# Where the receptance product R of a step is placed, in a convolution and channel-mix kernel on one core

## The chip, the cores and the metric

The kernel runs on one core of one Trainium2 chip. The metric is device time in microseconds (us) of that core, from the first to the last instruction with what starting and ending the program adds; lower is better. The profile is one execution taken by the hardware profiler; its span is a little shorter than the time that is measured without it. Five engines work side by side, each on its own list of instructions: TensorE (PE, with its weight loads PEld), VectorE (DVE), ScalarE (ACT), GpSimd (POOL) and SyncE (SP, which here only issues transfers).

## The reference

The input x has 8 sequences of 4160 positions with 192 channels. First comes a causal convolution of 7 taps, with the softmax of 8 rows of weights (one for each group of 24 channels). Its result y goes through a channel mix, in which each position is also mixed with the position before it:

```python
xk = mu_k * y + (1.0 - mu_k) * y_prev
xr = mu_r * y + (1.0 - mu_r) * y_prev
k = np.maximum(xk @ w_k, 0.0)          # 192 -> 1024
v = k * k @ w_v                        # 1024 -> 192
r = 1.0 / (1.0 + np.exp(-(xr @ w_r)))  # 192 -> 192
out = r * v
```

## The kernel before

**Layout.** Two sequences are worked on together (a pair p of four), one in partitions 0 to 63 and one in 64 to 127 of the 128. The convolved y of a pair lies transposed, channels by positions, in the tile yT.

**Steps.** A step s is 512 positions of a pair. The first pair begins with a step of 256 (step 0) and ends with one of 256 (step 8); the other pairs have eight steps of 512. The last 64 positions of all pairs form a last step, number 33 (LAST). In a step, VectorE makes the difference `d` of neighbouring positions (`diff`, L480), scales it by mu (`scale`, L516) and adds y (`add_y`, L522), once into xk and once into xr. The tiles xk and xr have two buffers each, which the steps take in turn.

**Products.** K of a step comes in 8 slots (4 in a step of 256 positions); a slot is 128 rows of the 1024 for both sequences, in one PSUM tile of two banks. `k_mm` (L542) multiplies, `k_relu` (L554, ScalarE) takes it into the tile k_sb, which has four buffers, and `k_square` (L568, VectorE) squares it into k2. V and R are made for 256 positions at a time (j counts them): `r` (L599) and `r_out` (L610, the sigmoid on ScalarE), `v_rows` (L630) in two halves, and `v_out` (L646, VectorE), which multiplies V by R and starts the stores.

**PSUM.** All of K, R, V and the convolution share one ring of four PSUM tiles (`ring`, tag "k"). A tile is held from its first matmul until ScalarE or VectorE has read it. V's is held longest, until `v_out` at the beginning of the next bundle.

**Bundles.** The order of the work is written out by hand and kept by each engine. Four K slots make a bundle; there are 65, counted from 0, so that a step of 512 positions has two bundles and step 8 has bundle 15 alone. `first_bundle[s]` and `last_bundle[s]` say where a step's K lies. V of a pair of halves is due one bundle after its step's last K, one V in a bundle: this is `vb` in the list `quads`. A bundle from the fourth on (`bundle_rest`) runs in this order: the squares left over, the lists `mix_a`, V's output of the bundle before, two K with their relus, `mix_b`, two squares, `mix_c`, the third K, the R products of list `rq`, V's first half, a square, the fourth K, convolution pieces in some bundles, V's second half. The sigmoids of the list `rs` stand ahead of V's first half in bundles with convolution pieces, and behind it in the others.

Into these lists go, for a step s with first bundle fb, the difference in the bundle fb - 2 as a rule, xk's work in fb - 1, and the scaling of xr in `mix_c` of fb - 1, then in fb:

```python
at(mix_c, fb - 1, scale, s, 1, 0)
at(mix_a, fb, scale, s, 1, 1)
```

R of the pair (s, j) is put into a bundle by one line, and V by `vb`:

```python
b = min(vb, last_bundle[s] + 1 + j) if s else vb
at(rq, b, r, s, j)
at(rs, b, r_out, s, j)
```

Around step 8 this gives:

| pair (s, j) | vb | bundle of R before |
|---|---|---|
| (6, 0), (6, 1) | 13, 14 | 13, 14 |
| (7, 0), (7, 1) | 15, 16 | 15, 16 |
| (8, 0) | 17 | 16 |
| (9, 0), (9, 1) | 18, 19 | 18, 19 |

**Convolution.** Most of y is made by TensorE from the loaded x (L302), copied out by ScalarE (L319), written to a buffer in DRAM (L424) and read back transposed into yT (L432). In the first bundles the convolution of the first pair still goes on.

Of the kernel before, what the change touches and what calls it, by code (L numbers as in the profile page):

```python
# [14 lines left out]
def kernel(  # L15
# [56 lines left out]
    T0, LAST = S - TAIL, len(steps) - 1  # L72
# [11 lines left out]
    first_bundle = [bundle_of[st[3]] for st in steps]  # L84
    last_bundle = [bundle_of[st[3] + st[4] - 1] for st in steps]
# [202 lines left out]
    def conv_tiles(g, c):  # L288

        nb = groups[g][2]  # L290
        if c == 0:
            ys[g] = two.tile([P, GB, 2 * D], BF16, tag="y", name="y")
        ps = ring.tile([P, 2, BANK], FP32, tag="k", name="ps_c")
        conv_ps[g, c] = ps
        m = nb // 2
        banks = ps[:, :, 0 : m * 4 * G].rearrange("p i (m s c) -> p i m s c", m=m, s=2)
        for k in range(2):
            h = 2 * c + k
            for i in range(2):
                q = slice(i * Q, (i + 1) * Q)  # L300
                for j in range(2):
                    nc.tensor.matmul(  # L302
                        out=banks[j * Q : (j + 1) * Q, i, :, :, k * G : (k + 1) * G],
                        lhsT=toe[q, h, q],
                        rhs=xbs[g][q, j * m : (j + 1) * m, :, h * G : (h + 1) * G],
                        start=True,
                        stop=True,
                    )

    def conv_tiles_out(g, c):  # L310

        m = groups[g][2] // 2
        ps = conv_ps.pop((g, c))
        y = ys[g]
        c0, c1 = 2 * c * G, 2 * (c + 1) * G
        cuts = [c0] + [a for a in range(Q, D, Q) if c0 < a < c1] + [c1]
        for a, b in zip(cuts, cuts[1:]):
            d = a // Q * 2 * Q + a % Q
            nc.scalar.copy(  # L319
                out=bass.AP(  # L320
                    tensor=y.tensor,
                    offset=y.offset + d,
                    ap=[y.ap[0], [m * 2 * D, 2], [2 * D, m], [Q, 2], [1, b - a]],
                ),
                in_=bass.AP(
                    tensor=ps.tensor,
                    offset=ps.offset + a - c0,
                    ap=[ps.ap[0], [BANK, 2], [4 * G, m], [2 * G, 2], [1, b - a]],
                ),
            )  # L330
# [195 lines left out]
    def k_mm(n, cs=range(NC)):  # L526


        s, j = slots[n]
        L = steps[s][2]  # L530
        xk = xks[s]
        if cs[0] == 0 and n not in k_ps:
            k_ps[n] = ring.tile([P, 2, BANK], FP32, tag="k", name="ps_k")
        ps = k_ps[n]
        nf = STEP // L

        for c in cs:
            for f in range(nf):
                fs = slice((j * nf + f) * P, (j * nf + f + 1) * P)
                for i in range(2):  # L540
                    r = slice(i * Q, (i + 1) * Q)
                    nc.tensor.matmul(  # L542
                        out=ps[:, i, f * L : (f + 1) * L],
                        lhsT=wk[r, c, fs],
                        rhs=xk[r, c, :L],
                        start=c == 0 and f == 0,
                        stop=c == NC - 1 and f == nf - 1,
                    )

    def k_relu(n):  # L550
        ps = k_ps.pop(n)
        k_sb = four.tile([P, 2 * STEP], BF16, tag="k_sb", name="k_sb")
        k_sbs[n] = k_sb
        nc.scalar.activation(out=k_sb, in_=ps.rearrange("p a b -> p (a b)"), func=AF.Relu)  # L554

    def k_square(n):
        s, j = slots[n]
        L = steps[s][2]
        k_sb = k_sbs.pop(n)
        if j == 0:  # L560
            k2s[s] = three.tile([P, NF, 2 * STEP], BF16, tag="k2", name="k2")
        nf = STEP // L
        i = k_sb
        o = k2s[s][:, j, :]
        if nf > 1:
            i = k_sb.rearrange("p (b f t) -> p f b t", b=2, f=nf)
            o = k2s[s][:, j * nf : (j + 1) * nf, 0 : 2 * L].rearrange("p f (b t) -> p f b t", b=2)
        nc.vector.tensor_tensor(out=o, in0=i, in1=i, op=ALU.mult)  # L568
# [3 lines left out]
    vb = 1  # L572
    for s, (p, t0, L, n0, ns) in enumerate(steps):
        for j in range(L // 256):
            vb = max(vb, last_bundle[s]) + 1
# [44 lines left out]
    def v_rows(s, j, half, ks=(0, 1)):  # L620

        if half == 0:
            v_ps[s, j] = ring.tile([P, 2, BANK], FP32, tag="k", name="ps_v")[:, :, 0 : 2 * D]
        for k in ks:
            for f in range(NF):
                for i in range(2):
                    q = slice(i * Q, (i + 1) * Q)
                    bank = (i + half) % 2
                    t = tile_of(s, j, 2 * bank + k)
                    nc.tensor.matmul(  # L630
                        out=v_ps[s, j][:, bank, k * D : (k + 1) * D],
                        lhsT=k2s[s][q, f, t * P : (t + 1) * P],
                        rhs=wv[q, f, :],
                        start=half == 0 and k == 0 and f == 0,
                        stop=half == 1 and k == 1 and f == NF - 1,
                    )
        if half == 0:
            nc.scalar.clobber_nop([nc.scalar.lower_ap(v_ps[s, j])])
# [4 lines left out]
    def v_out(s, j):  # L643
        p, t0, L, _, _ = steps[s]
        o_sb = three.tile([P, 4, D], FP32, tag="o_sb", name="o_sb")
        nc.vector.tensor_tensor(  # L646
            out=o_sb.rearrange("p (b t) d -> p b (t d)", b=2),
            in0=v_ps.pop((s, j)),
            in1=r_sbs.pop((s, j)),
            op=ALU.mult,  # L650
        )
        for st in range(2):
            c = t0 + 2 * j * P
            nc.sync.dma_start(
                out=out[2 * p + st, c : c + 2 * P, :].rearrange("(m p) d -> p m d", p=P),
                in_=o_sb[:, 2 * st : 2 * st + 2, :],
            )
# [24 lines left out]
    early, rq, rs, xt, mix_a, mix_b, mix_c, vq, late = ({} for _ in range(9))  # L682

    def at(table, b, fn, *a):
        table.setdefault(b, []).append((fn, a))
# [7 lines left out]
    for g, (p, base, nb, fb, on_pe) in enumerate(groups):  # L693
# [12 lines left out]
        if g > 4:  # L706

            b = {5: 1, 6: 2, 7: 7}.get(g)
            b = first_bundle[first_step[p]] + (-15, -11, -7, -3)[(g - 6) % 4] if b is None else b
# [30 lines left out]
        if s == LAST - 1 or s < LAST and steps[s + 1][0] > p:  # L740
            at(late, fb - 1, keep_tail, p)
    for s, j, vb in quads:
        b = min(vb, last_bundle[s] + 1 + j) if s else vb
        at(rq, b, r, s, j)
        at(rs, b, r_out, s, j)
        if s == LAST:
            at(late, vb, v_last, s, j)
        else:
            vq.setdefault(vb, []).append((s, j))

    def run(table, b):
        for fn, a in table.get(b, ()):
            fn(*a)
# [114 lines left out]
    def bundle_rest(b, ns):  # L868

        units = xt.get(b, [])  # L870
        quad = vq[b][0]
        for n in bundles[b - 1][2 if b == 3 else 3 :]:
            k_square(n)
        run(mix_a, b)
        if b > 3:
            v_out(*vq[b - 1][0])
        k_mm(ns[0])
        k_relu(ns[0])
        k_mm(ns[1])
        k_relu(ns[1])  # L880
        run(mix_b, b)
        k_square(ns[0])
        k_square(ns[1])
        run(mix_c, b)
        k_mm(ns[2])
        k_relu(ns[2])
        run(rq, b)
        if units:
            run(rs, b)
        v_rows(*quad, 0)  # L890
        if not units:
            run(rs, b)
        k_square(ns[2])
        k_mm(ns[3])
        k_relu(ns[3])
        for u in units:
            conv_tiles(*u)
            conv_tiles_out(*u)
        v_rows(*quad, 1)
        run(late, b)  # L900
# [87 lines left out]
```

## Time and profile before

| | |
|---|---|
| time, median of 3 | 417.65 us (417.5 to 418.0) |
| span of the profiled execution | 415.7 us, TensorE clock 0.998 of full |
| TensorE busy | 404.4 us, 97% |
| TensorE weight loads busy | 301.3 us, 72% |
| VectorE busy | 369.5 us, 89% |
| ScalarE busy | 354.9 us, 85% |
| one K matmul, one V or R matmul (mean) | 367 ns, 243 ns |
| relu, sigmoid (ScalarE) | 1036 ns, 821 ns |
| square, V's output (VectorE) | 687 ns, 952 ns |

Lines of the timeline give the start and the length in us, the engine, the line of the code, the operation with the tile that it writes and those that it reads, how many instructions are joined in the line, and in brackets how long the engine stood idle before it and what it waited for. The ends of matmuls are modelled and they overlap, so their distances are best taken from start to start. The chain of waits is the chain of work that ended last, followed back from the end; its lines give start, length and what ran or waited there.

### The profile page before, as it was taken

The page shows a single profiled execution, that of the slowest core. Times are in us where ns is not written, and L with a number is a line of the kernel's source. Part 1 is how long each engine was busy: PE and PEld are TensorE (multiplying, and loading weights), DVE is VectorE, ACT ScalarE, POOL GpSimd, SP SyncE. Part 2 cuts the span into 40 slices and gives each one's busy share as a digit, 9 for nine tenths or more (in the row PEclk, how much of TensorE's full clock was granted, in tenths as well). Part 3 has the DMA queues.
Part 4 walks back from the last instruction along what each step waited for, and adds up shares of the span by engine and source line. Part 5 has one row for each costly group of instructions (what it writes and reads, how often), then busy time and mean ns, then how long its engine had stood idle before and what let it go on. Part 6 is the DMA issues. An engine that isn't in the chain of part 4 may idle for free.

```text
span 415.7 us, 16804 instructions
## 1 busy us (share of the span) xinstructions
PE 404.4 (97%) x7349; PEld 301.3 (72%) x7350; DVE 369.5 (89%) x671; ACT 354.9 (85%) x429; POOL 65.2 (16%) x102
## 2 busy tenths in 40 slices
PE   7899999999889999999999999999999999999996
PEld 5567767777667777767777777777777777777895
DVE  5989799999699999989989999998989899999973
ACT  6899988888868889988888988888898888787781
POOL 8750023021040200304031020303100000000000
PEclk9999999999999999999999999999999999999999
DMA  9999989969559795999759797796962726411223
GB/s 148 175 191 213 187 184 213 241 133 193 151 102 231 137 225 139 155 191 155 192 122 229 180 148 195 108 235 131 204 168 80 209 73 160 121 53 65 79 79 114
DMA packets 137657, 65.58 MB, mean 158 GB/s; under 512 B 87388, under 2 KB 137584, under 8 KB 137584
## 3 DMA queue, kind: packets, MB, share of 16 engines
q1 hardware_dynamic: 95840, 48.42, 44.6%
q0 software_dynamic: 40944, 15.53, 32.9%
q8 instruction: 57, 0.93, 0.9%
q10 hardware_dynamic: 800, 0.57, 0.5%
q14 instruction: 16, 0.13, 0.1%
HBM read 31.62 MB, written 37.09 MB: 165 GB/s over the span
## 4 chain that ended last, share of the span: by engine, by line
PE 85%; DMA 5%; DVE 3%; ACT 2%; POOL 2%; issue 1%; SPq 0%; ACTq 0%; DVEq 0%; POOLq 0%
PE ps_v L630 38%; PE ps_k L542 35%; PE ps_r L599 7%; PE ps_c L302 3%; DMA xb<-in_x_dram 2%; DMA yT<-y_dram 2%; PE ps_v L582 1%; DMA y_dram<-y 1%; DVE k L568 1%; POOL xb L136 1%; ACT k_sb L554 1%; POOL wk L208 1%; ACT y L319 1%; DVE o_sb L646 1%; DMA out_dram<-o_sb 1%
## 5 line engine op out<-in xcount | busy, mean ns | idle before, releaser
L554 ACT ACTIVATE k_sb<-ps_k 128x1024 bf16<-128x1024 f32 x260 | 253.2, 1036 | 36.8 <-PE ps_k L542 34.6
L568 DVE TENSOR_TENSOR k<-k_sb 128x1024 bf16<-128x1024 bf16 x260 | 172.9, 687 | 28.3 <-ACT k_sb L554 27.9
L542 PE MATMUL ps_k<-xk,wk 64*128 64x512 bf16 (+1 forms) x1632 | 191.1, 367 | 0.9 <-DVE xk L522 0.5
L630 PE MATMUL ps_v<-wv,k 64*128 64x192 bf16 x4032 | 188.2, 243 | 2.4 <-ACT k_sb L554 1.4
L630 PEld LDWEIGHTS <-k 64*128 64x128 bf16 x4032 | 168.0, 94 | 16.2 <-issue 7.0
L542 PEld LDWEIGHTS <-wk 64*128 64x128 bf16 x1632 | 80.3, 94 | 59.3 <-issue 1.3
L136 POOL DMA_DIRECT2D xb<-in_x_dram x62 | 45.1, 736 | 175.4 <-issue 81.5
L646 DVE TENSOR_TENSOR o_sb<-ps_v,r_sb 128x768 f32<-128x768 f32 x64 | 61.0, 952 | 3.1 <-issue 2.4
L610 ACT ACTIVATE r_sb<-ps_r 128x768 bf16<-128x768 f32 x65 | 53.2, 821 | 12.0 <-PE ps_v L630 11.3
L319 ACT CAST y<-ps_c 128x960 bf16<-128x960 f32 (+5 forms) x84 | 50.8, 686 | 0.0
L599 PEld LDWEIGHTS <-xr 64*128 64x128 bf16 x780 | 34.5, 94 | 16.0 <-issue 2.2
L599 PE MATMUL ps_r<-wr,xr 64*128 64x192 bf16 x780 | 43.1, 243 | 0.9 <-DVE o_sb L646 0.6
L516 DVE TENSOR_SCALAR xr<-d,mu 128x512 bf16<-128x512 bf16 (+1 forms) x102 | 35.1, 351 | 3.8 <-PE ps_r L599 3.8
L480 DVE TENSOR_TENSOR d<-yT 128x1536 bf16<-128x1536 bf16 (+3 forms) x37 | 31.5, 854 | 1.4 <-ACT yT L381 0.9
L522 DVE TENSOR_TENSOR xr<-xr,yT 128x1536 bf16<-128x1536 bf16 (+1 forms) x33 | 31.0, 939 | 1.1
L516 DVE TENSOR_SCALAR xk<-d,mu 128x512 bf16<-128x512 bf16 (+1 forms) x98 | 31.8, 353 | 0.1
L522 DVE TENSOR_TENSOR xk<-xk,yT 128x1536 bf16<-128x1536 bf16 (+2 forms) x34 | 30.6, 901 | 0.1
L302 PEld LDWEIGHTS <-toe 64*64 64x64 bf16 x448 | 9.6, 106 | 11.6 <-issue 10.8
L302 PE MATMUL ps_c<-xb,toe 64*64 64x240 bf16 (+1 forms) x448 | 16.6, 265 | 0.1
L464 POOL COPY y_tail<-yT 128x195 bf16<-128x195 bf16 x4 | 2.8, 698 | 65.0 <-DMA yT<-y_dram 64.9
L111 POOL MEMSET xb<- 32x384 bf16 x3 | 1.3, 423 | 43.2 <-DVE xb L109 43.2
L371 PEld LDWEIGHTS <-xb 128*32 128x32 bf16 (+3 forms) x264 | 4.6, 106 | 2.3 <-issue 1.0
(59 smaller groups left out, 65.0 us busy)
## 6 DMA issues: line engine op xcount, KB each, us to landing
out_dram<-o_sb SPq DMA_DIRECT2D x128, 192.0 KB
xb<-in_x_dram POOLq DMA_DIRECT2D x40, 240.0 KB, 8.1
y_dram<-y SPq DMA_DIRECT2D x44, 210.0 KB
y_dram<-y SPq DMA_DIRECT2D x12, 168.0 KB
xb<-in_x_dram POOLq DMA_DIRECT2D x10, 192.0 KB, 5.6
xb<-in_x_dram POOLq DMA_DIRECT2D x6, 216.0 KB, 6.9
xb<-in_x_dram POOLq DMA_DIRECT2D x6, 144.0 KB, 5.6
wk<-in_moe_w_k_dram POOLq DMA_DIRECT2D x4, 96.0 KB, 4.7
```

The lines of the kernel that those rows point to most:

```text
L136: nc.gpsimd.dma_start(out=xb[q0 : q0 + rows, lo:hi, s, :], in_=bass.AP(tensor=x.tensor, offset=x.offset + (b * S + t0 + lo * step) * D, ap ...
L302: nc.tensor.matmul(out=banks[j * Q : (j + 1) * Q, i, :, :, k * G : (k + 1) * G], lhsT=toe[q, h, q], rhs=xbs[g][q, j * m : (j + 1) * m, :, ...
L319: nc.scalar.copy(out=bass.AP(tensor=y.tensor, offset=y.offset + d, ap=[y.ap[0], [m * 2 * D, 2], [2 * D, m], [Q, 2], [1, b - a]],), in_=bas ...
L516: nc.vector.tensor_scalar(out=t[:, c, :L], in0=diffs[s][:, c, :L], scalar1=mu[:, i, c : c + 1], scalar2=None, op0=ALU.mult)
L522: nc.vector.tensor_tensor(out=o, in0=o, in1=y_of(s, sl, 0), op=ALU.add)
L542: nc.tensor.matmul(out=ps[:, i, f * L : (f + 1) * L], lhsT=wk[r, c, fs], rhs=xk[r, c, :L], start=c == 0 and f == 0, stop=c == NC - 1 and f ...
L554: nc.scalar.activation(out=k_sb, in_=ps.rearrange("p a b -> p (a b)"), func=AF.Relu)
L568: nc.vector.tensor_tensor(out=o, in0=i, in1=i, op=ALU.mult)
L599: nc.tensor.matmul(out=ps[:, i, k * D : (k + 1) * D], lhsT=xr[q, c, ts], rhs=wr[q, c, :], start=c == 0, stop=c == NC - 1,)
L610: nc.scalar.activation(out=r_sbs[s, j], in_=r_ps.pop((s, j))[:, :, 0 : 2 * D], func=AF.Sigmoid)
L630: nc.tensor.matmul(out=v_ps[s, j][:, bank, k * D : (k + 1) * D], lhsT=k2s[s][q, f, t * P : (t + 1) * P], rhs=wv[q, f, :], start=half == 0 ...
L646: nc.vector.tensor_tensor(out=o_sb.rearrange("p (b t) d -> p b (t d)", b=2), in0=v_ps.pop((s, j)), in1=r_sbs.pop((s, j)), op=ALU.mult,)
```

## The change

Two edits. The first gives R another rule: it may not be later than the two bundles in front of the first bundle of the second next step, one R in each, which is when the xr buffer is wanted again; without that bound it goes with its V, and the last step's R goes one bundle ahead of it. The second moves V's output in bundle 4, the fifth, ahead of the left-over square and of the scaling in `mix_a`, so that the PSUM tile of V is read earlier there; in all later bundles the order stays.

```diff
     for s, j, vb in quads:
-        b = min(vb, last_bundle[s] + 1 + j) if s else vb
+        b = vb - (s == LAST)
+        if 0 < s < LAST - 1:
+            b = min(b, first_bundle[s + 2] - 2 + j)
         at(rq, b, r, s, j)
         at(rs, b, r_out, s, j)
...
         units = xt.get(b, [])
         quad = vq[b][0]
+        if b == 4:
+            v_out(*vq[b - 1][0])
         for n in bundles[b - 1][2 if b == 3 else 3 :]:
             k_square(n)
         run(mix_a, b)
-        if b > 3:
+        if b > 4:
             v_out(*vq[b - 1][0])
```

## The prediction

> **What bounds the kernel now.** I read the page's first two parts, then the engines' busy time in stretches of two bundles, then the timeline of each engine where a stretch came out long, then the chain of waits. Bundles are counted from 0, so the fifth is bundle 4; R(s,j) and V(s,j) are the two products of pair j of step s.
>
> ```profile
> PE 404.4 (97%) x7349; PEld 301.3 (72%) x7350; DVE 369.5 (89%) x671; ACT 354.9 (85%) x429; POOL 65.2 (16%) x102
> ```
>
> TensorE is the bound: 97% busy. But the average hides one bad place. Each line below is two bundles, from the second half of V in one odd bundle to that in the next (11 to 13, 13 to 15, 15 to 17, 17 to 19); the columns are start and end, length, busy time of PE, PEld, DVE, ACT and POOL with their instructions, clock and transfers.
>
> ```profile
> 83.97:96.08 12.11, 12.11 (x218) 8.91 (x220) 11.11 (x22) 10.85 (x14) 4.64 (x7) 1.00 0.78 141
> 96.08:108.38 12.30, 12.29 (x242) 10.10 (x244) 11.43 (x23) 10.84 (x14) 0.00 (x0) 1.00 0.85 195
> 108.38:123.47 15.09, 12.71 (x220) 9.10 (x220) 11.22 (x21) 10.96 (x14) 4.03 (x7) 1.00 0.46 101
> 123.47:135.50 12.03, 12.03 (x218) 8.87 (x220) 11.73 (x22) 10.77 (x14) 0.41 (x1) 1.00 1.10 228
> ```
>
> The third has the same 48 K, 128 V, 24 R and 16 convolution matmuls as its neighbours and takes 3.0 us more (15.09 against 12.03 to 12.11). After 123 us the table of waits has no wait of TensorE at all, so whatever is saved ahead of that should arrive whole at the end. The timeline of the long stretch, VectorE first:
>
> ```profile
> 107.59 0.95 DVE L522 TENSOR_TENSOR xk<-xk,yT 128x1536 bf16<-128x1536 bf16 x1
> 112.38 0.35 DVE L516 TENSOR_SCALAR xr<-d,mu 128x512 bf16<-128x512 bf16 x1 [3.83 <-PE ps_r L599]
> 112.64 1.28 DVE L568 TENSOR_TENSOR k<-k_sb 128x1024 bf16<-128x1024 bf16 x2
> ...
> 114.11 0.95 DVE L646 TENSOR_TENSOR o_sb<-ps_v,r_sb 128x768 f32<-128x768 f32 x1
> ...
> 119.79 0.95 DVE L646 TENSOR_TENSOR o_sb<-ps_v,r_sb 128x768 f32<-128x768 f32 x1
> ```
>
> VectorE stands still for 3.83 us in front of the first scaling of xr for step 9. There are two xr buffers; step 9's is step 7's, and R(7,1) still has to read it. R(7,1) is bound to bundle 16, the scaling to the end of bundle 15. Behind the scaling, in order, wait the squares of bundle 15 and the V output of bundle 15. What this does to TensorE:
>
> ```profile
> 111.67 0.67 PE L599 MATMUL ps_r<-wr,xr 64*128 64x192 bf16 x12
> 112.58 0.67 PE L599 MATMUL ps_r<-wr,xr 64*128 64x192 bf16 x12 [0.25 <-ACT k_sb L554]
> 114.50 1.50 PE L630 MATMUL ps_v<-wv,k 64*128 64x192 bf16 x32 [1.24 <-ACT k_sb L554]
> ...
> 120.79 1.50 PE L630 MATMUL ps_v<-wv,k 64*128 64x192 bf16 x32 [0.89 <-DVE o_sb L646]
> ```
>
> Matmul ends are modelled, so I count from start to start. One R takes 0.50 (99.28 to 99.78), a half of V 1.32, three K blocks 1.94 (97.34 to 99.28). Against that the second R of bundle 16 is late by 0.41 (111.67 + 0.50 to 112.58), V by 1.42 (113.08 to 114.50), and V of bundle 17 by 1.07 (117.78 + 1.94 to 120.79; there is no R in bundle 17). Sum 2.9 to 3.0, the whole excess. The middle one goes through ScalarE: the relu at 113.42 waited 0.89 for a square, since its four k_sb buffers were full.
>
> The other place that the change touches is bundles 4 to 7. R of bundle 4 starts 2.33 after its first K (35.20 to 37.53) where 1.94 is usual: 0.39 of waiting for the V output. The chain of waits does not go through it:
>
> ```profile
> 37.96 4.73 DMA y_dram<-y
> ...
> 42.85 7.12 DMA yT<-y_dram
> ...
> 49.99 0.98 DVE d L480
> ```
>
> **What the Trainium skill says.** "Perfetto Trace Analysis", section on the Tensor Engine instruction, has ScalarE and VectorE as strict first-in-first-out queues, with TensorE's matmul end only estimated. The trace agrees on the first: the squares ready since about 109 us ran only at 112.64, behind the scaling. "PSUM — Partial Sum Buffer", section on engine versus sequencer instructions, says that matmuls start and complete in program order; so one R that lacks a buffer holds V and the next K blocks, as at 112.58 and 114.50. "Perfetto Trace Analysis", section on the most-contended engine, prefers weight-load busy time to matmul busy time as a measure of headroom. That is 72% here, yet the steady stretches show TensorE without a gap; I take the start-to-start times as its floor.
>
> **The change part by part: the R binding.** Worked out over all steps, the old and the new rule give the same bundle for every pair but two. Steps take two bundles, so the first bundle of step s+2, less 2, is just where R already is, except around step 8, which has 256 positions and one bundle (15). There R(7,0) goes from bundle 15 to 14, and R(7,1) from 16 to 15. R(8,0) stays in 16 and bundle 17 has none. So bundle 14 now has two R, bundle 16 one. The last step's R stays in bundle 65 (old minimum of 66 and 65, new 66 less 1). No instruction is added or removed.
>
> Gain: in bundle 15, R runs at about 105.2 and VectorE comes to the scaling at 108.5, so the wait of 3.83 goes. With it go the waits in bundles 16 and 17: 0.41 + 1.42 + 1.07 to 1.19, about 3.0 us.
>
> Cost: bundle 14 gets a second R and a second sigmoid. The R itself, 0.50 of TensorE, is only moved. For PSUM, R needs the slot of the V output (ended 98.50), the second R that of the first K (its relu ended about 99.2, R comes at 99.78) and V that of the second K (about 100.2, V comes at 100.28): no wait, with nothing to spare. The sigmoid is on the path:
>
> ```profile
> 101.38 0.81 ACT L610 ACTIVATE r_sb<-ps_r 128x768 bf16<-128x768 f32 x1 [0.24 <-PE ps_v L630]
> 102.08 1.02 ACT L554 ACTIVATE k_sb<-ps_k 128x1024 bf16<-128x1024 f32 x1
> ```
>
> The relu of the fourth K block follows 0.70 after a sigmoid. With the second R and sigmoid it starts at 102.08 + 0.50 + 0.70 = 103.3 and ends at 104.3. Behind it on VectorE stand its square, two scalings and the V output of bundle 14, whose end was 2.05 after the relu's (103.10 to 105.15), so it ends at about 106.4. R of bundle 15 took that slot: it starts at 105.20, just after 105.15, about 0.2 late. Unhindered it would come at 105.0 + 0.5 = 105.5; it waits until 106.4. That is 0.9 late where it was 0.2, a cost of 0.7.
>
> Does the lag go on? VectorE would be some 1.2 late, its xk for step 9 ends at 108.54 + 1.2 = 109.8, and the first K of bundle 16 comes at 109.65 + 1.2 = 110.9: no wait. The V output of bundle 15 ends near 112.5, R of bundle 16 comes near 112.8: no wait. Bundle 17 then has the timing of any other odd bundle, in which the V output ends 1.89 after the first K (90.96 to 92.85), against 1.94 for the matmul behind it. So the cost stays at 0.7. Its ends are 0 (the allocator gives R another slot) and 1.6 (V of bundle 14 has to take the third K's slot, whose relu ends at 101.14, and is another 0.9 late). Net: 3.0 less 0.7 is 2.3.
>
> **The V output in bundle 4.** VectorE's order there was two squares (35.06), the scaling of xk, the V output (36.53 to 37.48). Ahead of the second square and the scaling it can start near 35.7 and end at 36.65, before R would come (37.14), so R's 0.39 goes; the square loses 0.95, but its consumers are a bundle away. But the difference at 49.99 waits for the transposing read that landed at 49.97, and that chain begins with convolution copies at 34.22 and writes queued from 36.21, both of bundle 3. The output's stores, which could disturb it, were queued behind these writes (39.36, long after the output's end). The first K of bundle 7 waits for the xk made from this difference (ends 53.94, matmul 54.06). A TensorE that is 0.39 early waits 0.39 longer there. I take 0, with 0.4 as the other end.
>
> **The rivals.** *A full gain*: R of bundle 15 gets another slot, or bundle 4 arrives after all: 2.9 to 3.4 us, 414.2 to 414.8. For it: slots seem to go to what was freed first, and in bundle 16 R did not take the late V output's slot. Against: R did so in bundles 4, 7 and 15. *A new wait takes half*: the chain through the second sigmoid, or V in bundle 14, costs 1.6, or 1.2 to 2.1 with 0.4 to 0.5 to either side: 417.65 less 0.9 to 1.8, 415.9 to 416.8. For it: nothing is to spare in bundle 14. Against: the V output of bundle 13 is out at 98.50, well ahead of the first R at 99.28, so its slot should serve. *No change*: the stall only moves by one bundle, 417.0 to 418.4; against it stands that bundle 15's R comes 3 us ahead of the scaling. *Slower*: the crowded bundle 14 delays VectorE so that xk of step 9 comes late too, and the late k_sb releases stall the relus, as happened in bundle 16; three waits of 1.4, 1.4 and 1.2 in place of 3.0 would give 418.7. Against it: VectorE's lag of 1.2 is a third of the 3.83 that caused the old ones.
>
> **How the numbers follow.** 417.65 less 2.3 is 415.35, rounded to 415.3 (55%). Full gain 20%, half 12%, no change 8%, slower 5%. Faster by over 0.2% (0.84 us) are the first three, 87%. The range 414.2 to 416.8 holds these three and with them both ends of the unknown costs; no change and slower, 13%, stay outside but for the edge of the former.
>
> **What would show it.** Right: no wait of VectorE for ps_r, the stretch from bundle 15's V to bundle 17's V near 12 us, the R of bundle 15 just behind the end of the V output of bundle 14 with VectorE some 1.2 late, and the difference of step 4 still released by the transposing read near 50 us. Wrong: a wait of TensorE over 1 us between 97 and 106, any repeating gap after 123, or the first K of bundle 7 well before 54.

## The result, and the profile after

| | before | after |
|---|---|---|
| time, median of 4 | 417.72 us (417.5 to 418.0) | 415.5 us (414.75 to 415.84) |
| span of the profiled execution | 415.7 us | 414.1 us |

The ratio is 0.9944, 95% interval 0.9927 to 0.9961: faster by 2.2 us. On five further rounds, beside other kernels, the changed kernel had a ratio of 0.9940 (0.9925 to 0.9955).

First the page's busy times of the changed kernel, then its busy times in two stretches. The second is the stretch from the second half of V in bundle 15 to that in bundle 17, the one that took 15.09 us before.

```profile
PE 404.1 (98%) x7349; PEld 302.2 (73%) x7350; DVE 369.1 (89%) x671; ACT 355.0 (86%) x429; POOL 65.9 (16%) x102
```

```profile
98.01:110.20 12.19, 11.48 (x224) 9.52 (x221) 10.21 (x21) 10.22 (x13) 0.00 (x0) 1.00 0.73 173
110.20:121.81 11.61, 11.61 (x208) 8.41 (x205) 11.21 (x22) 10.14 (x13) 4.41 (x7) 1.00 0.78 120
```

The sum of TensorE's work has hardly changed (404.1 against 404.4); what has gone is idle time, in the stretch 2.38 us of it (15.09 less 12.71 busy). The stretch is down to 11.61 us with TensorE busy in all of it: 12.1 less one R, which has moved to bundle 14. The first stretch, bundles 14 and 15 up to that V, now holds 0.71 us of idle (12.19 less 11.48). The timeline of TensorE shows both:

```profile
99.95 1.15 PE L599 MATMUL ps_r<-wr,xr 64*128 64x192 bf16 x24
...
104.23 2.15 PE L542 MATMUL ps_k<-xk,wk 64*128 64x256 bf16 x36
107.09 0.67 PE L599 MATMUL ps_r<-wr,xr 64*128 64x192 bf16 x12 [0.71 <-DVE o_sb L646]
...
117.26 2.11 PE L542 MATMUL ps_k<-xk,wk 64*128 64x512 bf16 x18
119.20 1.50 PE L630 MATMUL ps_v<-wv,k 64*128 64x192 bf16 x32
```

At 99.95 stand the two R of bundle 14, 24 matmuls in one line. In bundle 17 V follows the first K by 1.94, unhindered (3.01 before, 117.78 to 120.79). In exchange R of bundle 15 comes 2.86 after the first K, where it was 2.14 in the kernel before:

```profile
103.06 2.13 PE L542 MATMUL ps_k<-xk,wk 64*128 64x256 bf16 x36
105.20 0.67 PE L599 MATMUL ps_r<-wr,xr 64*128 64x192 bf16 x12
```

Why, ScalarE and VectorE of the changed kernel tell:

```profile
102.56 1.51 ACT L610 ACTIVATE r_sb<-ps_r 128x768 bf16<-128x768 f32 x2 [0.74 <-PE ps_v L630]
103.95 4.01 ACT L554 ACTIVATE k_sb<-ps_k 128x1024 bf16<-128x1024 f32 x4
```

```profile
105.02 0.69 DVE L568 TENSOR_TENSOR k<-k_sb 128x1024 bf16<-128x1024 bf16 x1 [1.25 <-ACT k_sb L554]
...
106.08 0.95 DVE L646 TENSOR_TENSOR o_sb<-ps_v,r_sb 128x768 f32<-128x768 f32 x1
...
109.47 0.95 DVE L522 TENSOR_TENSOR xk<-xk,yT 128x1536 bf16<-128x1536 bf16 x1
110.34 0.35 DVE L516 TENSOR_SCALAR xr<-d,mu 128x512 bf16<-128x512 bf16 x1
```

Two sigmoids (x2) delay the relu behind them; VectorE waits 1.25 us for it and the V output ends at 107.03, 0.06 ahead of R. The scaling at 110.34, the one that stood 3.83 us before, follows the xk addition at once: R(7,1), which reads the buffer that this scaling overwrites, has already run at 107.09.

The profile's span fell by 1.6 us only. The profiles cut into pieces at the same matmuls show why:

| kernel | start to first K of bundle 4 | from there to R of bundle 7 | from there to second half of V, bundle 17 | the rest |
|---|---|---|---|---|
| before | 35.20 | 21.39 | 66.81 | 292.3 |
| after | 36.22 | 21.04 | 64.55 | 292.3 |

The first column holds no changed instruction. It varies between profiles of one and the same kernel (36.22 here, 35.20 in another profile of the changed kernel), so this execution merely started 1.0 us late. The third column has the gain, 2.26 us.

### The profile page after: what moved, and what is told of

The parts are those of the page before. It is cut to its first block, busy times and chain, and to the rows that moved or that the text cites. A ratio compares the mean times of both kernels' runs of the same rounds, so it can differ in the third digit from the quotient of the medians.

```text
span 414.1 us, 16805 instructions
## 1 busy us (share of the span) xinstructions
PE 404.1 (98%) x7349; PEld 302.2 (73%) x7350; DVE 369.1 (89%) x671; ACT 355.0 (86%) x429; POOL 65.9 (16%) x102
## 4 chain that ended last, share of the span: by engine, by line
PE 84%; ACT 3%; DMA 3%; DVE 2%; issue 1%; SPq 1%; ACTq 0%
PE ps_v L630 37%; PE ps_k L542 35%; PE ps_r L599 7%; PE ps_c L302 3%; DMA yT<-y_dram 2%; ACT k_sb L554 2%; PE ps_v L582 1%; ACT y L319 1%; DMA y_dram<-y 1%; DVE k L568 1%; DMA out_dram<-o_sb 1%; DVE o_sb L646 0%; ACT r_sb L610 0%; SPq L424 0%; DVE xk L522 0%
```

## The experiments

All in five rounds. A time is the median; ratios are against the kernel before on the same chip. "Columns" are those of the table above, in its order.

**R alone, and V's output alone.** In the first, only the lines of the R binding are changed, in the second only these:

```diff
+        if b == 4:
+            v_out(*vq[b - 1][0])
...
-        if b > 3:
+        if b > 4:
             v_out(*vq[b - 1][0])
```

> The kernel before with the new R binding alone; V's output in bundle 4 stays where it was. Theory (all of the gain is the xr wait around bundle 16, and bundle 4's part is absorbed by the transposing read): the gain of the whole change, ratio about 0.9945 (415.4 us), no wait of VectorE for ps_r, R of bundle 15 about 0.7 us late, and from the first K of bundle 7 to the second half of V in bundle 17 the same 67.1 us as in the changed kernel. Rival (V's output in bundle 4 brings its 0.4 us): 0.4 us slower than the whole change, about 415.9 us.

> The kernel before with V's output moved in bundle 4 alone; R stays bound as before. Theory (absorbed): R of bundle 4 starts 1.94 us after its first K in place of 2.33, the difference of step 4 still starts when the transposing read lands, and the time stays within 0.2 us of 417.7. Rival (it carries through): 417.3 us, with the first K of bundle 7 some 0.4 us earlier after the convolution copies of bundle 3.

R alone: 415.18 us, ratio 0.9943 (0.9929 to 0.9957), columns 35.75, 20.82, 64.55. The third is that of the changed kernel to the digit, and the wait of R in bundle 15 is 0.71 too: this part carries the whole of the 2.26. The distance that the expectation named, from the first K of bundle 7 to V of bundle 17, missed: it is 66.51 (54.61 to 121.12) and not the 67.1 of the changed kernel (67.13, 54.68 to 121.81). The next paragraphs say what lies between.

V's output alone: 417.33 us, ratio 0.9991 (0.9984 to 0.9998), columns 36.05, 20.72, 66.82. R of bundle 4 follows its first K by 1.94 as foreseen, and the first K of bundle 7 comes 18.46 after that of bundle 4, against 18.86 in the kernel before and in R alone. So the 0.4 does reach bundle 7's K. How much of it gets past bundle 7's R is another matter. VectorE's difference of step 4 in R alone, and behind it the R that it leads to:

```profile
49.97 0.96 DVE L480 TENSOR_TENSOR d<-yT 128x1536 bf16<-128x1536 bf16 x1
```

```profile
54.61 2.11 PE L542 MATMUL ps_k<-xk,wk 64*128 64x512 bf16 x18
56.57 0.67 PE L599 MATMUL ps_r<-wr,xr 64*128 64x192 bf16 x12
```

The same in the changed kernel:

```profile
50.66 0.96 DVE L480 TENSOR_TENSOR d<-yT 128x1536 bf16<-128x1536 bf16 x1 [0.54 <-DMA yT<-y_dram]
```

```profile
54.68 2.11 PE L542 MATMUL ps_k<-xk,wk 64*128 64x512 bf16 x18
57.26 0.67 PE L599 MATMUL ps_r<-wr,xr 64*128 64x192 bf16 x12 [0.47 <-DVE o_sb L646]
```

In both, R starts 6.60 after the difference (49.97 to 56.57, 50.66 to 57.26), and it is 6.60 or 6.61 in all eight profiles in which R and V's output of bundle 7 stand where they stand here. In R alone the difference waits for nothing and R comes 1.96 after the first K. With the edit VectorE arrives earlier and waits for the transposing read, and R waits in turn. In the kernel before, both waited as well: the difference at 49.99 for the read, and R for the V output.

```profile
54.06 2.11 PE L542 MATMUL ps_k<-xk,wk 64*128 64x512 bf16 x18
56.59 0.67 PE L599 MATMUL ps_r<-wr,xr 64*128 64x192 bf16 x12 [0.43 <-DVE o_sb L646]
```

So what is left of the 0.4 hangs on when the read lands. The second column is 20.8 to 21.4 in the three kernels without the edit and 20.7 to 21.0 in the five with it and no other edit in bundles 5 to 7; the means are 21.06 and 20.81. The ranges overlap, and most of the difference of the means comes from one late read, that in the profile of the kernel before (without it the first mean is 20.90). The times do not settle it either. A time of 417.33 and a first K of bundle 7 that is 0.40 earlier are what the rival of V's output alone forecast, and the interval, 0.1 to 0.7 us, just excludes a gain of nothing; but R alone is not 0.4 slower than the whole change, as the same rival had it (0.9943 against 0.9944 and 0.9940). Whether none, some or all of the 0.4 stays is not shown.

**A third buffer for xr, with R where it was.**

```diff
-            (xks, xrs)[i][s] = two.tile([P, NC, STEP], BF16, tag=("xk", "xr")[i], name=("xk", "xr")[i])
+            (xks, xrs)[i][s] = (two, three)[i].tile([P, NC, STEP], BF16, tag=("xk", "xr")[i], name=("xk", "xr")[i])
```

> The kernel before with three xr buffers in place of two; R stays bound as before, so bundle 16 still has two R. If the shared xr buffer is the cause of the 3.83 us wait, it disappears though no R has moved, the three waits of TensorE behind it (0.41, 1.42 and 1.07 to 1.19 us) go, and the second sigmoid now costs its 0.7 us one bundle pair later, as a wait of V in bundle 17 for the V output of bundle 16: about 2.3 us of gain, 415.4 us. Rival (it is the two R in one bundle that stop TensorE, whatever VectorE does): the waits in bundles 16 and 17 stay above 2 us and the time above 417 us.

415.59 us, ratio 0.9950 (0.9936 to 0.9964), columns 35.60, 20.97, 64.55. First VectorE and then TensorE of this kernel:

```profile
107.57 0.95 DVE L522 TENSOR_TENSOR xk<-xk,yT 128x1536 bf16<-128x1536 bf16 x1
108.45 0.35 DVE L516 TENSOR_SCALAR xr<-d,mu 128x512 bf16<-128x512 bf16 x1
```

```profile
111.57 1.15 PE L599 MATMUL ps_r<-wr,xr 64*128 64x192 bf16 x24
...
115.85 2.12 PE L542 MATMUL ps_k<-xk,wk 64*128 64x512 bf16 x18
118.51 1.50 PE L630 MATMUL ps_v<-wv,k 64*128 64x192 bf16 x32 [0.54 <-DVE o_sb L646]
```

No R has moved, bundle 16 still has two in a row, and the wait of 3.83 is gone with the two waits of bundle 16. The cause was the shared buffer. The bundle behind the pair of R pays a price of the same size as in the changed kernel: V of bundle 17 comes 2.66 after the first K instead of 1.94, 0.72 late (that the second sigmoid is its cause was tested in the changed kernel only, in the next experiment). The two ways of freeing the buffer agree to 0.01 us in the third column.

**The second sigmoid behind the fourth relu of bundle 14, in the changed kernel.**

```diff
-        at(rs, b, r_out, s, j)
+        at(late if (s, j) == (7, 0) else rs, b, r_out, s, j)
```

> The changed kernel with the sigmoid of R(7,0) put behind the fourth relu of bundle 14 in place of ahead of it. Theory (the second sigmoid delays relu, square and V output of bundle 14, and with it R of bundle 15): the relu starts about 0.7 us earlier, the wait of R in bundle 15 falls from 0.71 to about 0, and the time falls by 0.6 to 0.7 us, to about 414.8 us. Rival (the R itself, or PSUM, delays it): the wait of 0.7 stays and the time stays at 415.4; or the PSUM tile that this R holds for longer makes a K of bundle 15 wait as long, and nothing is won.

414.45 us, ratio 0.9922 (0.9907 to 0.9936), columns 35.22, 20.78, 63.85. First ScalarE and then TensorE:

```profile
101.29 0.81 ACT L610 ACTIVATE r_sb<-ps_r 128x768 bf16<-128x768 f32 x1 [0.74 <-PE ps_v L630]
102.00 1.02 ACT L554 ACTIVATE k_sb<-ps_k 128x1024 bf16<-128x1024 f32 x1
102.91 0.82 ACT L610 ACTIVATE r_sb<-ps_r 128x768 bf16<-128x768 f32 x1
```

```profile
102.97 2.14 PE L542 MATMUL ps_k<-xk,wk 64*128 64x256 bf16 x36
105.12 0.67 PE L599 MATMUL ps_r<-wr,xr 64*128 64x192 bf16 x12
```

The relu follows the first sigmoid by 0.71 (103.95 - 102.56 = 1.39 in the changed kernel), and R of bundle 15 follows its first K by 2.15 (102.97 to 105.12) against 2.86. The third column falls by 0.70, which is this and nothing else: the second R and the longer hold on its PSUM tile cost no wait.

**V's output first in bundle 15 as well, in bundle 7 as well, and in both.** The list in the two conditions of the change becomes (4, 15), (4, 7) or (4, 7, 15):

```diff
-        if b == 4:
+        if b in (4, 7, 15):
             v_out(*vq[b - 1][0])
...
-        if b > 4:
+        if b > 3 and b not in (4, 7, 15):
             v_out(*vq[b - 1][0])
```

> The changed kernel with V's output first also in bundle 15, ahead of the left-over square and the scalings. Theory (R of bundle 15 waits 0.71 us because the V output stands on VectorE behind a square whose relu is late): the wait goes to 0 with the second sigmoid still where it was, 0.6 to 0.7 us faster than the changed kernel, about 414.8 us. Rival (the V output itself is late, V of bundle 14 having ended late): the wait stays.

> The changed kernel with V's output first also in bundle 7. Theory (the 0.4 us won in bundle 4 is lost in bundle 7, where R waits for the V output, which stands behind work that starts with the difference of step 4, which waits for the transposing read): the distance from the first K of bundle 4 to R of bundle 7, 20.7 to 21.0 us with bundle 4's edit and 20.8 to 21.4 without it, falls to 20.4 us, and the time by 0.3 to 0.6 us to about 415.0 us. Rival (TensorE is held at bundle 7 by xk itself, or later by the same read): the gain appears later as another wait and the time stays at 415.4 us.

> The changed kernel with V's output first in bundles 4, 7 and 15. If the two effects are what the single edits say, they add: no wait of R in bundles 4, 7 and 15, about 1.0 to 1.2 us faster than the changed kernel, 414.3 us. If one hides the other: no better than the better of the two.

| V's output first in | time | ratio | columns |
|---|---|---|---|
| 4, 15 | 414.36 us | 0.9912 (0.9899 to 0.9926) | 36.59, 20.80, 63.67 |
| 4, 7 | 415.04 us | 0.9929 (0.9915 to 0.9942) | 35.64, 20.44, 64.54 |
| 4, 7, 15 | 413.82 us | 0.9901 (0.9888 to 0.9915) | 35.55, 20.62, 63.66 |

With 15, R of that bundle follows its first K by 1.97:

```profile
104.36 2.15 PE L542 MATMUL ps_k<-xk,wk 64*128 64x256 bf16 x36
106.33 0.68 PE L599 MATMUL ps_r<-wr,xr 64*128 64x192 bf16 x12
```

The third column gains 0.88, the 0.71 and the 0.17 by which it was late before the change. The V output was not late itself; it stood behind a square whose relu was. With 7, the second column reaches 20.44, and R comes 1.95 after the first K. What comes near to bounding bundle 7 then is the first K itself (VectorE, then TensorE, of the kernel with 4 and 7):

```profile
50.12 0.96 DVE L480 TENSOR_TENSOR d<-yT 128x1536 bf16<-128x1536 bf16 x1 [0.58 <-DMA yT<-y_dram]
...
53.12 0.95 DVE L522 TENSOR_TENSOR xk<-xk,yT 128x1536 bf16<-128x1536 bf16 x1
```

```profile
54.13 2.12 PE L542 MATMUL ps_k<-xk,wk 64*128 64x512 bf16 x18
56.08 0.66 PE L599 MATMUL ps_r<-wr,xr 64*128 64x192 bf16 x12
```

K starts 0.06 after its xk is made and 1.35 after the half of V in front of it (52.78), only 0.03 more than where nothing holds it. In time, the edit in bundle 7 alone does not stand clear of the changed kernel's intervals; its column does. The third kernel has both gains, though in its profile the read came later (the difference waited 0.77 for it), and with it xk and the first K of bundle 7, which starts 1.54 after the half of V (52.68 to 54.22): 20.62 in place of 20.44.

**The double R in bundle 5, and that together with the three.** R of steps 2 to 7 goes one bundle earlier from R(2,1) on:

```diff
             b = min(b, first_bundle[s + 2] - 2 + j)
+        if 2 <= s <= 7 and (s, j) != (2, 0):
+            b = vb - 1
```

> The changed kernel with R of steps 2 to 7 one bundle earlier from R(2,1) on, so that the bundle with two R is bundle 5 and bundles 6 to 16 have one each. Theory (a second R costs only through its sigmoid, and only where the next bundle's R waits for the V output; and bundles 5 to 7 wait for the transposing read anyway): R of bundle 15 waits 0.2 us as before the change in place of 0.71, the R moved out of bundle 14 (0.50 us of TensorE) is hidden by the wait in bundle 7, sum 0.7 to 1.2 us, 414.2 to 414.7 us. Rival (the second R costs its 0.5 us and its sigmoid wherever it stands): 415.4 us as in the changed kernel.

> The changed kernel once more, on one chip with the next one, for their difference. As on its first runs: ratio about 0.9945, R of bundle 15 waits 0.71 us, R of bundle 7 0.2 to 0.6 us behind the difference of step 4.

> The double R in bundle 5 together with V's output first in bundles 4, 7 and 15. Theory (both edits remove the same waits, so they do not add; what is left is TensorE's own work): no wait of R in bundles 7 and 15, at most 0.2 us better than either alone, 413.7 us, 1.6 to 1.8 us below the changed kernel. Rival (moving R off bundle 14 frees ScalarE too and that was worth something by itself): 413.2 us or less.

| kernel | time | ratio | columns |
|---|---|---|---|
| double in 5 | 413.94 us | 0.9903 (0.9890 to 0.9917) | 35.42, 20.97, 63.35 |
| changed, again | 415.15 us | 0.9940 (0.9925 to 0.9955) | 35.20, 20.73, 64.55 |
| double in 5, output first in 4, 7, 15 | 413.90 us | 0.9902 (0.9888 to 0.9917) | 36.50, 20.96, 63.14 |

In the kernel with the double R in bundle 5 the third column falls by 1.20, the 0.50 of the R and some 0.7 of the wait behind it (R of bundle 15 follows its first K by 2.14, as before the change). The second column takes the 0.50 without growing beyond what it was, because R of bundle 7 no longer waits for the V output; it follows its first K by 1.95. The combination adds only 0.2 in the third column, as the theory had it, and nothing that the times can tell. These kernels, near 413.9 us, beat both the kernel before and the changed one. Four of the times lie 0.3 to 0.5 us under their forecasts (414.45, 414.36, 413.82 and 413.94, against 414.8, 414.8, 414.3 and 414.2 at the least), which is no more than the intervals are wide, 0.6 us to either side.

## Why the prediction was right

415.3 us was forecast and 415.5 measured, and all steps but the last of these ran as forecast. That the times agree to 0.2 us is luck in part, since the interval of the gain is 1.6 to 3.0 us; the distances in the profiles test the steps more sharply.

- *The cause of the stall.* Shown, by the third buffer: with the sharing taken away and R left alone, the wait of 3.83 and the two waits of bundle 16 went, and that of bundle 17 fell to the 0.7 that the second sigmoid was to cost.
- *The gain.* Put at 2.9 to 3.0 for three waits. All three are gone in the changed kernel; the stretch fell by 3.48 (15.09 less 11.61), and less the 0.50 of the R that moved away this is 2.98.
- *The cost through the second sigmoid.* Put at 0.7, as 0.9 against 0.2. R of bundle 15 is 0.89 late (2.86 less the 1.97 of an unhindered one) against 0.17. The working put the fourth relu at 103.3 and the end of the V output at 106.4; the changed kernel ran 0.67 later from bundle 14's first K (98.01 against 97.34), and with that taken off they were 103.28 and 106.36. The lag also ended where the working had it end: with the same 0.67 taken off, xk of step 9 was made at 109.75 and the first K of bundle 16 came at 110.86, without a wait (109.8 and 110.9 forecast). The sigmoid moved behind the relu gave the 0.7 back. The doubt about the slots was needless: R did take the V output's tile, and V of bundle 14 waited for nothing.
- *The net.* 2.3 forecast, 2.26 in the third column.
- *Bundle 4.* Put at 0, between ends of 0 and 0.4. The runs do not tell where between these ends it lies, and two reasons of that step failed. The first K of bundle 7 did not wait for xk before: it stood at 54.06, just 1.32 after the half of V in front of it (52.74), as any K does, and the end of xk at 53.94 was a near miss. What waited there was R, for a V output that let it start only 6.60 us behind the difference. And the transposing read is not a fixed time: in R alone the difference was not kept waiting by it. That gain is lost to this read is as forecast in kind; the place was another, and how much is lost differs with the read. V's output moved in bundle 7 showed the place.

What stays open: how much of the 0.4 of bundle 4 is kept, and what sets the time at which the read lands. An error of up to 0.4 us in this step would not show in the time of the whole change.

## What to carry to other kernels

When work with a rotating buffer is bound to a place by what consumes it, check the places where a short stage makes two rhythms differ: one reader left behind the next writer of its buffer stopped an in-order engine for 3.8 us and the bound engine for 2.9. The repair moves a second instruction into some other place, and its price is found there by walking one chain, from the extra instruction through every queue behind it to the first wait of the bound engine. Putting the tile-freeing instruction ahead of work that is itself waiting took that price away.

## What the runs showed that was not expected

The part ahead of the first K of bundle 4 took 35.20 to 36.59 us over all profiles, though nothing in it differs between the kernels, and 36.22 and 35.20 in two profiles of the same one. Its cause is not shown. This spread of 1.4 us is over half the effect that was studied; times of single profiles could not have settled it, distances between matmuls could, since the third column of the changed kernel, of R alone and of the third buffer repeated to 0.01 us. The transposing read, too, took 6.8 to 7.1 us from its start to the difference that waited for it (42.59 to 49.39 with the late sigmoid, 43.56 to 50.66 in the changed kernel). Since R of bundle 7 came 6.60 us behind that difference, it bore on how much of a gain of 0.4 us went on.
